# Decay attention and two feed-forward layers: the first activation from the Mish table, weight signs merged on VectorE

## The chip, the cores and the metric

The kernel runs on one core of a Trainium2 chip. The metric is the device time of one execution in microseconds, taken as the median of several runs; lower is better. The matrix engine is TensorE (PE in the profile, its weight loads PEld), the elementwise engines are VectorE (DVE), ScalarE (ACT) and GpSimd (POOL), and SyncE (SP) issues the transfers. Each engine works through its own queue in order, and semaphores make one wait for another.

## What is computed

Three things follow one another. First a causal attention with a decay, over 2 batches of 8 heads, 768 positions of 64 features; its output, put together, is 1536 tokens of 512 features. Then a feed-forward layer with Mish, `h = x @ w_in`, `g = h * tanh(log(1 + exp(h)))`, `g @ w_out`, with 2048 hidden features. Then a second such layer with `g = h * clip(h + 3, 0, 6) / 6`.

```python
def _moe_ref(x, w_in, w_out):
    h = x @ w_in
    sp = np.where(h > 20.0, h, np.log1p(np.exp(np.minimum(h, 20.0))))
    g = h * np.tanh(sp)
    return (g @ w_out).astype(np.float32)
```

The inputs and the result are float32, and the weights come to the chip as float64 bit patterns.

## The kernel before, in words

**Precision.** The large products run on float32r operands. To keep float32 accuracy each operand is split into a rounded high part (`split_hi`, a copy on ScalarE, L67) and the rest (`split_lo`, a subtraction on VectorE, L70). A product is then three matmuls: high by high, high by low, low by high.

**Tiles and steps.** Tokens are cut into three blocks `k` of 512 (X[k]), the hidden features into 16 tiles `t` of 128 (W[t], which holds a tile of the first matrix and of the second). A step `n` of the loop is one pair of layer and (k, t). There are 96 steps, 48 for each layer. In a step `gemm1` (L274, twelve matmuls of 512 columns) makes h for block k and tile t in PSUM, the activation makes g of it, and `gemm2` (L287, twelve matmuls) adds g times the second matrix into four PSUM banks y. The loop is pipelined by hand: in iteration n TensorE gets gemm1(n) and then gemm2(n-2). `act_first(n)` puts the first activation functions on ScalarE in the same iteration; `dve_first(n-1)`, `g_hi(n-1)` and `g_lo(n-1)` come an iteration later. h has two PSUM buffers, so gemm1(n+2) can start when the last reader of h(n) is done.

**The Mish activation before.** With th = tanh(h/2), Mish is a rational function of th. ScalarE makes th (L310), a square of it (L311) and, with Silu and Sin on scaled th (L312, L313), a first value for a reciprocal. VectorE makes a Newton step of it and the product with h (L322, L323, L324). L324 is the last reader of h. ScalarE then makes the high part of g (L334) and VectorE the low part (L342). The second layer uses Relu with a bias on ScalarE (L316), a minimum and product on VectorE (L328), and the plain splits.

**Weights.** A 64-bit pattern is turned into float32 in place in a staging tile `st`. A conversion (`convert`) has for a half of one tile W[t] (512 numbers wide) or of two tiles (1024 wide, seven times, the first ones after two narrow ones): on ScalarE a scaled copy of the high word (L247) and a copy of some low bits (L248); a merge of the sign; on VectorE a shift and merge (L258); then the split into W (L67 on ScalarE, L70 on VectorE). There are 57 conversions. The sign merge is done either on ScalarE (L253, a strided 16-bit write, with L248 writing 16-bit words) or on VectorE (L255, with L248 writing 32-bit words). A hand-written set `on_act` names 27 of the 57 for ScalarE. Two staging tiles alternate; a load of the next one is put on SP's queue (L236) after the conversion that frees its tile.

**Order.** The attention is done in 12 chunks. The first four come ahead of the loop; the others are threaded into iterations 0 to 15 by a table (`att_at`): `scores` makes a score product (L154), `weigh` masks it on VectorE, `attend` makes the outputs (L191, L197, L203), and `settle` moves these on. Another table (`conv_at`) says after which iteration how many conversions are put in, and `conv_first` whether ahead of the activation. The framework's planner may still move an instruction of a queue past others by its own estimate of when things are ready. The last four weight tiles, 12 to 15, lie where the attention's buffers were; each of the three blocks uses tiles 0 to 7 in steps 0 to 23 (block 2 goes on with 8 to 15 up to step 31), blocks 0 and 1 use 8 to 15 in steps 32 to 47, and the second layer runs over all 16 for each block in steps 48 to 95.

**Pools.** `g` (4 KB a partition) has two buffers, tm2 has two each for the tags `x`, `a` and `o` (2 KB), tm1 one for `th`. Output copies (L362) use tags `o` and `a` in turn, four buffers in all; the decay table's `lam_sb` and `pw` sit in `a` and `th`. One activation table set, with the functions of the first layer, is loaded at the start (L425).

Of the kernel before, what the change touches and what calls it, by code (L numbers as in the profile page):

```python
# [15 lines left out]
ALU = mybir.AluOpType  # L16
# [5 lines left out]
def decay_attention__mish_ffn__hswish_ffn_kernel(  # L22
# [18 lines left out]
    g_p = ctx.enter_context(tc.tile_pool(name="g", bufs=2))  # L41
# [21 lines left out]
    def f32(ap):  # L63
        return ap.bitcast(F32)
# [49 lines left out]
    def decay_tables():  # L114
        lam_sb = tm2_p.tile([128, 512], F32, tag="a", name="lam_sb")[0:8, 0:1]
        pw = tm1_p.tile([128, 512], F32, tag="th", name="pw")[0:8, 0:256]
# [187 lines left out]
    def act_first(n):  # L304
        h = h_t[n]
        x = tm2_p.tile([128, 512], F32, tag="x", name="x")
        if seq[n][0] == 0:
            th = tm1_p.tile([128, 512], F32, tag="th", name="th")
            a = tm2_p.tile([128, 512], F32, tag="a", name="a")
            nc.scalar.activation(out=th, in_=h, func=ACTF.Tanh, scale=0.5)  # L310
            nc.scalar.activation(out=x, in_=th, func=ACTF.Square, scale=-0.5, bias=0.5)  # L311
            nc.scalar.activation(out=a, in_=th, func=ACTF.Silu, scale=1.03356325, bias=-3.37153266)  # L312
            nc.scalar.activation(out=a, in_=a, func=ACTF.Sin, scale=-6.86865902, bias=0.1585412)  # L313
            f_t[n] = (x, a)
        else:
            nc.scalar.activation(out=x, in_=h, func=ACTF.Relu, bias=3.0)  # L316
            f_t[n] = x

    def dve_first(n):
        if seq[n][0] == 0:  # L320
            x, y0 = f_t[n]
            nc.vector.scalar_tensor_tensor(out=x, in0=x, scalar=1.0, in1=y0, op0=ALU.add, op1=ALU.mult)  # L322
            nc.vector.scalar_tensor_tensor(out=x, in0=x, scalar=-2.0, in1=y0, op0=ALU.add, op1=ALU.mult)  # L323
            nc.vector.scalar_tensor_tensor(out=x, in0=x, scalar=0.5, in1=h_t[n], op0=ALU.add, op1=ALU.mult)  # L324
            f_t[n] = x
        else:
            r = f_t[n]
            nc.vector.scalar_tensor_tensor(out=r, in0=r, scalar=6.0, in1=h_t[n], op0=ALU.min, op1=ALU.mult)  # L328
        del h_t[n]

    def g_hi(n):
        g = g_p.tile([128, 2, 512], F32R, tag="g", name="g")
        if seq[n][0] == 0:
            nc.scalar.activation(out=g[:, 0], in_=f_t[n], func=ACTF.Copy, scale=-2.0)  # L334
        else:
            split_hi(g[:, 0], f_t[n])
        g_t[n] = g

    def g_lo(n):
        g = g_t[n]  # L340
        if seq[n][0] == 0:
            nc.vector.scalar_tensor_tensor(  # L342
                out=g[:, 1], in0=f_t.pop(n), scalar=-2.0, in1=f32(g[:, 0]), op0=ALU.mult, op1=ALU.subtract
            )
        else:
            split_lo(g[:, 1], g[:, 0], f_t.pop(n))

    def evacuate(n, es):
        layer, k, t, first, last, end = seq[n]
        for e in es:  # L350
# [5 lines left out]
            elif end == "split":  # L356
                split_hi(X[k][:, 0, e, :], y)
                split_lo(X[k][:, 1, e, :], X[k][:, 0, e, :], y)
            else:
                o = tm2_p.tile([128, 512], F32, tag="o" if e % 2 else "a", name="o")  # L360
                r0 = k * 512 + e * 128
                nc.scalar.activation(out=o, in_=y, func=ACTF.Copy, scale=1.0 / 6.0)  # L362
                nc.sync.dma_start(out=out[r0:r0 + 128, :], in_=o)
# [49 lines left out]
    def advance(count):  # L413
# [7 lines left out]
    on_act = {  # L421
        0, 2, 3, 4, 5, 7, 9, 10, 11, 13, 14, 17, 19, 20, 21, 22, 35, 37, 44, 47, 48, 49, 50,
        51, 54, 55, 56,
    }
    nc.scalar.preload_act_table_set("silu_and_others")  # L425
# [146 lines left out]
```

## Time and profile before

| | |
|---|---|
| median of 3 runs | 616.82 us (616.25 to 617.41) |
| span of the profiled execution | 617.7 us |
| time of the profiled execution beyond its span | not given |
| TensorE, share of the span | 96% |
| ScalarE | 63% |
| VectorE | 55% |
| mean granted TensorE clock | 0.986 |

The span goes from the first to the last instruction on the core. Shares of an engine are means over stretches that differ, so they are to be read by stretch. A group of twelve matmuls of 512 columns is the unit of the work on TensorE; matmuls overlap, so the length of a group is best read from its start to the start of the next one.

### The profile page before, as it was taken

The numbers are of one execution on the slowest core, as the hardware profiler recorded it, in microseconds if no ns is written. First come the engines' busy times: TensorE is split into PE (matmuls) and PEld (weight loads), VectorE is DVE, ScalarE is ACT, GpSimd is POOL, SyncE is SP. The second block draws the span as 40 slices with busy tenths as digits, with TensorE's granted clock in tenths as the row PEclk, the third lists the DMA queues.
The fourth block names the chain that finished last, engine by engine and source line by source line (L and its number), as shares of the span: only waits on it lengthen the run. The fifth ranks groups of instructions, "written<-read, shape, count | busy, mean of one in ns | idle before, by whom it ended". The sixth has DMA issues, their size and how long they took to land.

```text
span 617.7 us, 7512 instructions
## 1 busy us (share of the span) xinstructions
PE 594.7 (96%) x2938; PEld 481.0 (78%) x2938; DVE 342.1 (55%) x527; ACT 388.3 (63%) x611; POOL 9.7 (2%) x14
## 2 busy tenths in 40 slices
PE   6989799999998999999999999999999999999997
PEld 3867577888776888878888888788888888888885
DVE  2776678778756888778797675522222222222221
ACT  0699989996899887898688977521322222322212
POOL 1400000000000000000000000000000000000000
PEclk8998899999999999999999999999999999999999
DMA  7935451441212323212212231100100000100001
GB/s 222 409 110 198 152 189 68 137 137 70 102 68 103 103 103 102 103 69 102 70 40 97 102 103 68 35 1 1 68 1 0 1 0 1 69 0 2 0 1 68
DMA packets 15955, 50.56 MB, mean 82 GB/s; under 512 B 1576, under 2 KB 3120, under 8 KB 15920
## 3 DMA queue, kind: packets, MB, share of 16 engines
q1 hardware_dynamic: 15920, 50.08, 23.1%
q8 instruction: 23, 0.38, 0.2%
q14 instruction: 12, 0.10, 0.1%
HBM read 46.92 MB, written 3.15 MB: 81 GB/s over the span
## 4 chain that ended last, share of the span: by engine, by line
PE 55%; ACT 29%; DVE 8%; DMA 5%; issue 3%; POOL 0%; SPq 0%; ACTq 0%; DVEq 0%; POOLq 0%
PE y L287 27%; PE h L274 26%; ACT st L248 6%; ACT st L253 5%; DMA st<-w 3%; ACT st L247 3%; ACT W L67 3%; ACT a L312 2%; ACT x L311 2%; ACT g L334 2%; ACT a L313 2%; ACT th L310 2%; DVE W L70 1%; DVE st L258 1%; ACT X L67 1%
## 5 line engine op out<-in xcount | busy, mean ns | idle before, releaser
L274 PE MATMUL h<-X,W 128*128 128x512 f32 x1152 | 285.2, 397 | 6.9 <-DVE x L324 5.4
L274 PEld LDWEIGHTS h<-X,W 128*128 128x128 f32 x1152 | 216.3, 189 | 58.4 <-DVE x L324 7.8
L287 PE MATMUL y<-g,W 128*128 128x512 f32 x576 | 141.6, 395 | 3.3 <-ACT W L67 2.7
L287 PE MATMUL y<-W,g 128*128 128x512 f32 x576 | 139.5, 391 | 0.1
L287 PEld LDWEIGHTS y<-g,W 128*128 128x128 f32 x576 | 109.0, 190 | 27.9 <-ACT W L67 3.1
L287 PEld LDWEIGHTS y<-W,g 128*128 128x128 f32 x576 | 108.0, 188 | 24.1 <-DVE g L70 0.7
L70 DVE TENSOR_TENSOR g<-x,g 128x512 fp32r<-128x512 f32 x48 | 33.2, 692 | 86.2 <-ACT g L67 86.2
L316 ACT ACTIVATE x<-h 128x512 f32<-128x512 f32 x48 | 28.8, 601 | 82.3 <-PE h L274 82.3
L67 ACT ACTIVATE g<-x 128x512 fp32r<-128x512 f32 x48 | 30.5, 634 | 78.0 <-PE y L287 77.1
L328 DVE SCALAR_TENSOR_TENSOR x<-x,h 128x512 f32<-128x512 f32 x48 | 33.0, 687 | 81.1 <-ACT x L316 81.1
L258 DVE SCALAR_TENSOR_TENSOR st<-st 128x512 int32<-128x512 int32 (+1 forms) x57 | 43.3, 761 | 37.9 <-ACT st L253 37.8
L248 ACT ACTIVATE st<-st 128x512 int32<-128x512 uint16 (+3 forms) x57 | 63.3, 1111 | 0.0
L70 DVE TENSOR_TENSOR W<-st,W 128x512 fp32r<-128x512 f32 (+1 forms) x57 | 43.8, 770 | 20.4 <-ACT W L67 19.6
L247 ACT ACTIVATE st<-st 128x512 f32<-128x512 f32 (+1 forms) x57 | 41.7, 732 | 9.7 <-DMA st<-w 9.6
L67 ACT ACTIVATE W<-st 128x512 fp32r<-128x512 f32 (+1 forms) x57 | 40.9, 719 | 5.7 <-DVE st L258 5.6
L342 DVE SCALAR_TENSOR_TENSOR g<-x,g 128x512 fp32r<-128x512 f32 x48 | 33.2, 691 | 19.1 <-ACT g L334 17.7
L253 ACT ACTIVATE st<-st 128x512 f16<-128x512 f32 (+1 forms) x27 | 42.5, 1576 | 0.4
L310 ACT ACTIVATE th<-h 128x512 f32<-128x512 f32 x48 | 30.0, 624 | 15.9 <-PE h L274 15.8
L334 ACT ACTIVATE g<-x 128x512 fp32r<-128x512 f32 x48 | 30.2, 629 | 9.2 <-DVE x L324 6.8
L322 DVE SCALAR_TENSOR_TENSOR x<-x,a 128x512 f32<-128x512 f32 x48 | 32.9, 686 | 4.9 <-ACT a L313 4.8
L323 DVE SCALAR_TENSOR_TENSOR x<-x,a 128x512 f32<-128x512 f32 x48 | 33.1, 689 | 0.9
L324 DVE SCALAR_TENSOR_TENSOR x<-x,h 128x512 f32<-128x512 f32 x48 | 32.8, 683 | 0.4
(42 smaller groups left out, 328.5 us busy)
## 6 DMA issues: line engine op xcount, KB each, us to landing
st<-w SPq DMA_DIRECT2D x50, 512.0 KB, 3.2
raw<-att SPq DMA_DIRECT2D x24, 512.0 KB, 4.8
st<-w SPq DMA_DIRECT2D x7, 1024.0 KB, 7.3
out<-o SPq DMA_DIRECT2D x12, 256.0 KB, 2.0
mask<-z SPq DMA_DIRECT2D x2, 256.0 KB, 3.9
table<-z SPq DMA_DIRECT2D x2, 128.0 KB, 4.4
lam_sb<-lam SPq DMA_DIRECT2D x1, 0.0 KB
z<-pw SPq DMA_DIRECT2D x1, 8.0 KB
```

What stands on the lines that cost most here:

```text
L67: nc.scalar.activation(out=hi, in_=src, func=ACTF.Copy)
L70: nc.vector.tensor_tensor(out=lo, in0=src, in1=f32(hi), op=ALU.subtract)
L247: nc.scalar.activation(out=hf, in_=hf, func=ACTF.Copy, scale=2.0 ** -112)
L248: nc.scalar.activation(out=lo16[..., 0] if sign_on_act else lo, in_=lo16[..., 1], func=ACTF.Copy, scale=2.0 ** -13, bias=2.0 ** -14 - 0.5,)
L253: nc.scalar.activation(out=sign, in_=hf, func=ACTF.Copy)
L258: nc.vector.scalar_tensor_tensor(out=hi, in0=hi, scalar=3, in1=lo, op0=ALU.logical_shift_left, op1=ALU.bitwise_or)
L274: nc.tensor.matmul(h, lhsT=W[t][:, a, kt * 128:kt * 128 + 128], rhs=X[k][:, b, kt, :], start=(kt, a, b) == order[0], stop=(kt, a, b) == or ...
L287: nc.tensor.matmul(y[e], lhsT=l, rhs=r, start=(first and i == 0), stop=(last and i == 2),)
L310: nc.scalar.activation(out=th, in_=h, func=ACTF.Tanh, scale=0.5)
L323: nc.vector.scalar_tensor_tensor(out=x, in0=x, scalar=-2.0, in1=y0, op0=ALU.add, op1=ALU.mult)
L334: nc.scalar.activation(out=g[:, 0], in_=f_t[n], func=ACTF.Copy, scale=-2.0)
L342: nc.vector.scalar_tensor_tensor(out=g[:, 1], in0=f_t.pop(n), scalar=-2.0, in1=f32(g[:, 0]), op0=ALU.mult, op1=ALU.subtract)
```

## The change

In the first layer the activation reads h twice from PSUM with the Mish function: once into x as float32 and once, rounded, into the high part of g. The low part is the plain subtraction. The four functions, the three VectorE operations and the scaled copy are gone for that layer; the second layer keeps its operations. `g` is now made in `act_first`, an iteration sooner, and has three buffers. The set `on_act` is empty, so all 57 sign merges are done on VectorE and L248 always writes 32-bit words. The tag `a` is gone: the output copies use two buffers of `o`, and `lam_sb` lies in `x`; `th` is half as long. The table set that is loaded at the start is the one with Mish.

```diff
--- before.py
+++ after.py
@@ -38,7 +38,7 @@
     NMID = 2
 
     main = ctx.enter_context(tc.tile_pool(name="main", bufs=1))
-    g_p = ctx.enter_context(tc.tile_pool(name="g", bufs=2))
+    g_p = ctx.enter_context(tc.tile_pool(name="g", bufs=3))
     tm2_p = ctx.enter_context(tc.tile_pool(name="tm2", bufs=2))
     tm1_p = ctx.enter_context(tc.tile_pool(name="tm1", bufs=1))
     dram_p = ctx.enter_context(tc.tile_pool(name="dram", bufs=1, space=DRAM))
@@ -112,8 +112,8 @@
         return rr.to_broadcast([128, 4, 2, 64])
 
     def decay_tables():
-        lam_sb = tm2_p.tile([128, 512], F32, tag="a", name="lam_sb")[0:8, 0:1]
-        pw = tm1_p.tile([128, 512], F32, tag="th", name="pw")[0:8, 0:256]
+        lam_sb = tm2_p.tile([128, 512], F32, tag="x", name="lam_sb")[0:8, 0:1]
+        pw = tm1_p.tile([128, 256], F32, tag="th", name="pw")[0:8, 0:256]
         nc.sync.dma_start(out=lam_sb, in_=lam.unsqueeze(1))
         load_raw(0, 0)
         load_raw(0, 1)
@@ -303,47 +303,28 @@
 
     def act_first(n):
         h = h_t[n]
+        g = g_p.tile([128, 2, 512], F32R, tag="g", name="g")
         x = tm2_p.tile([128, 512], F32, tag="x", name="x")
         if seq[n][0] == 0:
-            th = tm1_p.tile([128, 512], F32, tag="th", name="th")
-            a = tm2_p.tile([128, 512], F32, tag="a", name="a")
-            nc.scalar.activation(out=th, in_=h, func=ACTF.Tanh, scale=0.5)
-            nc.scalar.activation(out=x, in_=th, func=ACTF.Square, scale=-0.5, bias=0.5)
-            nc.scalar.activation(out=a, in_=th, func=ACTF.Silu, scale=1.03356325, bias=-3.37153266)
-            nc.scalar.activation(out=a, in_=a, func=ACTF.Sin, scale=-6.86865902, bias=0.1585412)
-            f_t[n] = (x, a)
+            nc.scalar.activation(out=x, in_=h, func=ACTF.Mish)
+            nc.scalar.activation(out=g[:, 0], in_=h, func=ACTF.Mish)
+            del h_t[n]
         else:
             nc.scalar.activation(out=x, in_=h, func=ACTF.Relu, bias=3.0)
-            f_t[n] = x
+        f_t[n] = x
+        g_t[n] = g
 
     def dve_first(n):
-        if seq[n][0] == 0:
-            x, y0 = f_t[n]
-            nc.vector.scalar_tensor_tensor(out=x, in0=x, scalar=1.0, in1=y0, op0=ALU.add, op1=ALU.mult)
-            nc.vector.scalar_tensor_tensor(out=x, in0=x, scalar=-2.0, in1=y0, op0=ALU.add, op1=ALU.mult)
-            nc.vector.scalar_tensor_tensor(out=x, in0=x, scalar=0.5, in1=h_t[n], op0=ALU.add, op1=ALU.mult)
-            f_t[n] = x
-        else:
+        if seq[n][0] == 1:
             r = f_t[n]
-            nc.vector.scalar_tensor_tensor(out=r, in0=r, scalar=6.0, in1=h_t[n], op0=ALU.min, op1=ALU.mult)
-        del h_t[n]
+            nc.vector.scalar_tensor_tensor(out=r, in0=r, scalar=6.0, in1=h_t.pop(n), op0=ALU.min, op1=ALU.mult)
 
     def g_hi(n):
-        g = g_p.tile([128, 2, 512], F32R, tag="g", name="g")
-        if seq[n][0] == 0:
-            nc.scalar.activation(out=g[:, 0], in_=f_t[n], func=ACTF.Copy, scale=-2.0)
-        else:
-            split_hi(g[:, 0], f_t[n])
-        g_t[n] = g
+        if seq[n][0] == 1:
+            split_hi(g_t[n][:, 0], f_t[n])
 
     def g_lo(n):
-        g = g_t[n]
-        if seq[n][0] == 0:
-            nc.vector.scalar_tensor_tensor(
-                out=g[:, 1], in0=f_t.pop(n), scalar=-2.0, in1=f32(g[:, 0]), op0=ALU.mult, op1=ALU.subtract
-            )
-        else:
-            split_lo(g[:, 1], g[:, 0], f_t.pop(n))
+        split_lo(g_t[n][:, 1], g_t[n][:, 0], f_t.pop(n))
 
     def evacuate(n, es):
         layer, k, t, first, last, end = seq[n]
@@ -357,7 +338,7 @@
                 split_hi(X[k][:, 0, e, :], y)
                 split_lo(X[k][:, 1, e, :], X[k][:, 0, e, :], y)
             else:
-                o = tm2_p.tile([128, 512], F32, tag="o" if e % 2 else "a", name="o")
+                o = tm2_p.tile([128, 512], F32, tag="o", name="o")
                 r0 = k * 512 + e * 128
                 nc.scalar.activation(out=o, in_=y, func=ACTF.Copy, scale=1.0 / 6.0)
                 nc.sync.dma_start(out=out[r0:r0 + 128, :], in_=o)
@@ -418,11 +399,8 @@
                 load_w(*plan[loaded[0]])
                 loaded[0] += 1
 
-    on_act = {
-        0, 2, 3, 4, 5, 7, 9, 10, 11, 13, 14, 17, 19, 20, 21, 22, 35, 37, 44, 47, 48, 49, 50,
-        51, 54, 55, 56,
-    }
-    nc.scalar.preload_act_table_set("silu_and_others")
+    on_act = set()
+    nc.scalar.preload_act_table_set("mish")
     warm_up(10)
     decay_tables()
     load_raw(2, 0)
```

## Rows read from the trace of the kernel before

**Rows 1.** Busy time of each engine over the whole span (the page's first part).

```profile
PE 594.7 (96%) x2938; PEld 481.0 (78%) x2938; DVE 342.1 (55%) x527; ACT 388.3 (63%) x611; POOL 9.7 (2%) x14
```

**Rows 2.** Busy us by stretch: PE, PEld, DVE, ACT, POOL (instructions), PEclk, DMA share, GB/s.

```profile
0.00:31.90 31.90, 24.70 (x242) 19.23 (x242) 16.71 (x35) 12.74 (x26) 9.67 (x14) 0.89 0.87 316
31.90:94.40 62.50, 55.67 (x331) 43.14 (x329) 44.36 (x60) 59.42 (x70) 0.00 (x0) 0.92 0.48 165
94.40:160.70 66.30, 66.30 (x424) 54.25 (x425) 52.59 (x81) 57.74 (x96) 0.00 (x0) 1.00 0.29 99
160.70:393.60 232.90, 227.68 (x986) 184.21 (x984) 171.97 (x270) 201.73 (x331) 0.00 (x0) 1.00 0.25 87
393.60:617.70 224.10, 220.31 (x960) 180.16 (x960) 56.47 (x82) 56.68 (x94) 0.00 (x0) 1.00 0.04 15
```

**Rows 3.** Waits of PE, whole span: us in total, times, longest us.

```profile
PE h L274 <- DVE x L324: 5.4, 7, 1.1
PE y L287 <- ACT W L67: 2.7, 1, 2.7
```

**Rows 4.** Chain that ended last, 31.9 to 94.4 us, shares by line.

```profile
by line: ACT st L248 20.9%; ACT st L253 19.1%; ACT W L67 10.0%; ACT st L247 8.3%; PE y L287 7.0%; ACT a L313 4.2%; ACT a L312 4.2%; DVE st L258 3.9%; ACT x L311 3.9%; ACT th L310 3.8%; ACT g L334 3.2%; ACT state L226 3.0%; issue 2.8%; ACT X
```

**Rows 5.** Timeline of PE, a group after a wait: start us, us, what.

```profile
45.28 5.46 PE L274 MATMUL h<-X,W 128*128 128x512 f32 x12 [0.60 <-DVE x L324]
```

**Rows 6.** Timeline of PE, the full stretch with attention.

```profile
100.09 1.16 PE L154 MATMUL sc<-raw 64*128 64x128 f32 x16
106.85 0.69 PE L191 MATMUL u<-raw 128*64 128x64 f32 x16
109.74 3.00 PE L274 MATMUL h<-X,W 128*128 128x512 f32 x12
...
145.99 1.16 PE L154 MATMUL sc<-raw 64*128 64x128 f32 x16
```

**Rows 7.** Timeline of PE (160.73, 393.56) and the chain's pieces (start us, us, what).

```profile
160.73 2.88 PE L274 MATMUL h<-X,W 128*128 128x512 f32 x12
...
393.56 3.02 PE L274 MATMUL h<-X,W 128*128 128x512 f32 x12 [0.44 <-DVE x L328]
...
201.32 2.72 PE y L287 x12
...
410.18 2.81 PE h L274 x12
```

**Rows 8.** Groups by line and shape: xcount, busy us, mean ns, idle before.

```profile
L253 ACT ACTIVATE st<-st 128x512 f16<-128x512 f32 x22 | 30.0, 1365 | 0.4
L310 ACT ACTIVATE th<-h 128x512 f32<-128x512 f32 x48 | 30.0, 624 | 15.9 <-PE h L274 15.8
L248 ACT ACTIVATE st<-st 128x512 uint16<-128x512 uint16 x22 | 29.8, 1356 | 0.0
L324 DVE SCALAR_TENSOR_TENSOR x<-x,h 128x512 f32<-128x512 f32 x48 | 32.8, 683 | 0.4
L248 ACT ACTIVATE st<-st 128x512 int32<-128x512 uint16 x28 | 18.7, 666 | 0.0
L253 ACT ACTIVATE st<-st 128x1024 f16<-128x1024 f32 x5 | 12.5, 2501 | 0.0
L248 ACT ACTIVATE st<-st 128x1024 uint16<-128x1024 uint16 x5 | 12.6, 2515 | 0.0
L255 DVE SCALAR_TENSOR_TENSOR st<-st 128x1024 int32<-128x1024 int32 x2 | 2.4, 1224 | 0.1
L248 ACT ACTIVATE st<-st 128x1024 int32<-128x1024 uint16 x2 | 2.3, 1140 | 0.0
L425 ACT ACT_TABLE_LOAD x1 | 1.3, 1283 | 0.7 <-PEq L564 0.7
```

**Rows 9.** Loads of wide staging tiles and output stores: KB each, us to landing.

```profile
st<-w SPq DMA_DIRECT2D x7, 1024.0 KB, 7.3
out<-o SPq DMA_DIRECT2D x12, 256.0 KB, 2.0
```

## The prediction, made before the change was run

> **What bounds the kernel now.** I read first the page's busy line [rows 1]: TensorE is busy for 594.7 of 617.7 us, so at first sight only 23.0 us are open. Next I cut the span into five stretches and asked for each engine's busy time in each [rows 2]. The cuts are the first matmul of L274 (31.9), the start of its eighth step (94.4), the end of the attention work (160.7), and the point at which the last weight has been converted (393.6). The reader should compare TensorE with ScalarE: from 31.9 to 94.4 TensorE idles 6.8 us and its granted clock is 0.92 while ScalarE is busy 59.4 of 62.5 us; from 94.4 to 160.7 TensorE never idles; from 160.7 to 393.6 it idles 5.2 us; after 393.6 it is full at clock 1.00 and ScalarE has 56.7 us in 224. TensorE's waits name VectorE's L324, the last of the three Newton and product steps, which frees a buffer of h, and a weight split on ScalarE [rows 3]. The chain of waits inside 31.9 to 94.4 shows what made those late: the two weight conversion lines L248 and L253 take 40.0% of it and the activation lines L310 to L334 over 19%, all on ScalarE [rows 4]. So TensorE bounds the kernel nearly everywhere, and ScalarE bounds it in two places.
>
> Idle time understates the loss, since a matmul at half the clock counts as busy: twelve matmuls of L274 took 5.46 us from 45.28 [rows 5], after a wait, against 2.72 us from start to start in a full stretch [rows 7]. I therefore count by full-speed periods. In the full stretch one score, one attend and two whole steps repeat; three of these periods go from 100.09 to 145.99, 15.30 us each [rows 6]. Between 31.9 and 94.4 lie seven gemm1 and five gemm2 groups, twelve in all, which is three periods' worth (four groups each), with three scores and four attends. The fourth attend is 2.89 us whole (106.85 to 109.74 [rows 6]), but of the four one has no carry and another no state product; I count 1.46 us. Needed: 45.90 + 1.46 = 47.4 us. Taken: 62.5. **Loss one: 15.1 us.** Between gemm1 of step 16 at 160.73 and of step 57 at 393.56 lie 41 steps in 232.83 us [rows 7]. At 5.44 us a step (two groups of 2.72) they need 223.0. Groups on the last four weight tiles take 2.81 instead of 2.72 even in the full stretch (the row at 410.18 [rows 7]); 12 of the 41 steps use those, 24 groups by 0.09, 2.2 us that stay. **Loss two: 232.8 - 223.0 - 2.2 = 7.6 us.**
>
> The Trainium skill (Perfetto Trace Analysis, Identifying the Most-Contended Engine) holds that matmul busy time is a poor measure of headroom and weight-load busy time a better one. By it, 481.0 us of weight loads at the last stretch's share, 180.16 of 224.1, would need 598 us, some 19.5 less than now, where the idle time of the two lossy stretches alone gives 12; the count by periods, 22.7, sides with the rule.
>
> **The change, part by part.**
> *Activation.* Per step of the first FFN ScalarE loses Tanh, Square, Silu, Sin and the scaled copy, five operations like the 0.624 us of L310, and gains two reads of h from PSUM; L310 is such a read, so 1.25 us: 3.12 - 1.25 = 1.87 us less. VectorE loses three operations and keeps one of four, at 0.683 us [rows 8], 2.05 us less. Over 48 steps: ScalarE -90 us, VectorE -98 us. In place of five functions, three VectorE steps and a copy in series there are two functions and one subtraction.
> *What h waits for.* h was freed by L324; now by the second Mish. From the end of gemm1(n) to the start of gemm1(n+2), which needs that buffer, TensorE has three groups, 8.2 us; the pair needs 1.25. The 5.4 us of waits on L324 [rows 3] therefore go, and no other operation takes their place until ScalarE is 6.9 us behind.
> *New waits.* The second Mish writes g at once, so g is held a step longer; the third buffer pays for it: the buffer that g(n) takes was read by gemm2(n-3), issued ahead of gemm1(n). x(n) waits for the subtraction of step n-2, as before. Cost nothing, covered by the 8.2 us.
> *Signs.* Of 27 sign merges on ScalarE five are 1024 wide, 2.50 us each, and 22 are 512 wide, 1.37 us. With the merge on VectorE, L248 also writes whole words: 2.52 becomes 1.14 us at 1024, 1.36 becomes 0.67 at 512. ScalarE: 5 x 3.88 + 22 x 2.06 = 65 us less. VectorE: 5 x 1.22 + 22 x 0.69 = 21 us more (the narrow ones priced like L324) [rows 8].
> *By stretch.* From 31.9 to 94.4, seven steps and five wide conversions: ScalarE 59.4 - 13.1 - 19.4 = 26.9 us, VectorE 44.4 - 14.4 + 6.1 = 36.1, against TensorE's need of 47.4. From 160.7 to 393.6, 32 steps and 16 conversions: ScalarE 201.7 - 59.8 - 33.0 = 109, VectorE 172.0 - 65.6 + 11.0 = 117, against 225. Neither engine can bound either stretch by its sum.
> *What is late next.* Weights. A wide conversion is six operations in series (three on each engine) of about 1.14 to 1.22 us, 7.1 us; its load of 1 MB lands after 7.3 us [rows 9]; two staging tiles alternate, and SP issues the next load only when the conversion two earlier has released its tile. That is 14.4 us for two conversions, 7.2 each, where TensorE needs the seven wide ones spread over its 47 us, 6.8 each, with two already loaded at the start. It just about keeps pace. I leave 3 of the 15.1 us there: bounds 0 (conversions always ahead) and 7.5 (half of the loss stays). Loss one gives 12.1 us.
> *Loss two* came from h and from ScalarE behind loads of 512 KB; I leave 0.6, bounds 0 and 3.8, since a conversion in ScalarE's queue still can hold a Mish until its load lands. Gain 7.0 us. No DMA is added or moved; loads start sooner as conversions end sooner.
> *Ahead of 31.9* the first conversion, narrow, stands among the first attention chunks: ScalarE loses 1.37 + 0.69 = 2.06 us, VectorE, busy too, gets 0.69. No row tells how much is on the path: bounds -2.06 and +0.69; I take the middle, -0.7.
> *Output and set-up.* Output copies alternate over two buffers instead of four, so the third of each four waits for the first one's transfer, 2.0 us [rows 9] less the copies between. The banks that they read are wanted a gemm1 later, 2.72 us. Taken 0, bound +1.3 for two places. lam and pw only change their tiles: 0.
> *Sum:* 617.7 - 0.7 - 12.1 - 7.0 = 597.9 us. This is against the profiled execution, of which only the span, 617.7, is given; the runs' median is 616.82, 0.14% less. Scaled so: **597.0 us**.
>
> **Rivals.**
> *Weights stay late.* The two-tile round trip just reckoned, or VectorE's three operations per conversion behind one another, keeps half of loss one, and loads keep half of loss two. For it: 14.4 us per pair is close to the need, and ScalarE already waits in its queue for splits. Against it: ScalarE's 40% of the chain [rows 4] is mostly the part that shrinks. 617.7 - 7.5 - 3.8 = 606.4, on the median 605.5.
> *Slower: table switches.* There is one table load now, 1.283 us, for a set with all four functions [rows 8]. If the Mish table came without Copy or Relu, each passage between Mish and a copy would cost a load on ScalarE. ScalarE has 319 us of work from 31.9 to 393.6 and loses 155, so it has room for 198 us, 154 loads, 3.2 per step. Two per step would leave it near no gain, since each stands ahead of a Mish; at four per step, as conversions are threaded between, 246 us, it would overrun by 48: 666 us. The Trainium skill (ScalarE: Activation LUTs, Table sets: the hidden batching unit) says that cheap functions, copy and relu among them, are in every set as filler, by which this does not happen; it does not list a set with Mish, and no row before shows one.
> *Nothing moves.* The same waits remain by another name, for example because ScalarE's queue, ordered by the planner, sits behind loads in both stretches: about 617. Against it: ScalarE's sums fall by half, and after 94.4, where it is busy 87% and not behind, TensorE never waits.
>
> **How the numbers follow.** Forecast 0.67; weights stay late 0.25; nothing moves 0.03; slower 0.05, most of it the switches. What a measurement here tells from no change is about 0.2%, 1.2 us. Faster 0.92, same 0.03, slower 0.05. The low end takes every best bound: 617.7 - 2.1 - 15.1 - 7.6 = 592.9, on the median 592. The high end is the first rival with the worst bounds of the opening and the outputs, 605.5 + 0.7 + 1.3 = 607.5. The range 592 to 607.5 leaves out the last two cases and little more.
>
> **What would show it.** Right: in the changed profile ScalarE about 27 us busy in the first seven steps and TensorE's granted clock there near 1.00; no wait of L274 on an activation step; that stretch about 50 us long; gemm1 of step 16 to step 57 about 226 us; from there to the end as before, 224 us. Weights late shows as waits of L274 and L287 on W. Switches show as more than one table load. The forecast is wrong if the stretch from 31.9 keeps over 55 us, or if the opening grows.

## The result, and the profile after

The changed kernel took **598.45 us** (median of 4 runs, 597.28 to 599.25), the kernel before on the same chip 617.12 (616.25 to 617.78). The ratio is **0.9686**, 95% interval 0.9657 to 0.9715: faster by 3.1%. The prediction was 597.0, in a range of 592 to 607.5. The profiled execution has a span of 596.9 us and took 599.02 in all, so about 2.1 us lie around the span.

The busy line of the page, as in [rows 1]:

```profile
PE 585.4 (98%) x2938; PEld 477.1 (80%) x2938; DVE 277.8 (47%) x410; ACT 255.8 (43%) x440; POOL 9.7 (2%) x14
```

ScalarE lost 132 us and VectorE 64; TensorE's instructions are the same in number and 9.3 us shorter in busy time. That alone does not explain a span that is 20.8 us shorter, so the stretches come next, cut at the same matmuls as [rows 2] (start, first matmul of L274, the start of its eighth step, the end of the attention work, the start of step 57). The columns are those of [rows 2]:

```profile
0.00:31.40 31.40, 23.86 (x242) 18.37 (x242) 17.52 (x36) 10.97 (x25) 9.69 (x14) 0.95 0.89 320
31.40:81.50 50.10, 49.93 (x331) 39.74 (x330) 43.11 (x52) 35.27 (x50) 0.00 (x0) 1.00 0.57 200
81.50:147.70 66.20, 66.20 (x426) 54.16 (x425) 39.12 (x59) 32.41 (x61) 0.00 (x0) 1.00 0.32 111
147.70:373.00 225.30, 225.30 (x985) 184.80 (x984) 123.96 (x187) 122.20 (x215) 0.00 (x0) 1.00 0.26 88
373.00:596.90 223.90, 220.13 (x961) 180.08 (x959) 54.07 (x79) 54.99 (x90) 0.00 (x0) 1.00 0.04 15
```

Read the first number behind each colon against [rows 2]: 31.4 for 31.9, **50.1 for 62.5**, 66.2 for 66.3, **225.3 for 232.9**, 223.9 for 224.1. The two stretches named in the prediction gave 20 of the 20.8 us. In both TensorE is now busy from end to end but for 0.2 us, and in the second row its granted clock is 1.00 (the 2.4 GHz level) where it was 0.92. The same matmuls fill 49.93 us there instead of 55.67 [rows 2]: groups at half clock, like the one of [rows 5], are gone, and this difference of 5.7 us is most of the 9.3.

TensorE's waits over the whole span (total us, times, longest), which answer to [rows 3]:

```profile
PE o L197 <- DVE amat L179: 4.5, 2, 3.3
PE sc L154 <- DMA raw<-att: 1.4, 1, 1.4
PE wp L84 <- DVE wz L81: 1.2, 1, 1.2
PE u L191 <- POOL raw L170: 0.5, 1, 0.5
PE y L287 <- ACT W L67: 0.2, 1, 0.2
```

All but the last belong to the opening. The 5.4 us on the last Newton step are gone, and of the 2.7 us on a weight split 0.2 is left. The chain of waits inside 31.4 to 81.5, by line, answers to [rows 4]:

```profile
by line: PE h L274 30.7%; PE y L287 22.8%; PE o L197 11.3%; PE sc L154 6.7%; PE o L203 6.5%; DVE st L258 4.6%; ACT W L67 4.6%; PE u L191 2.5%; DVE st L255 2.4%; ACT st L248 2.1%; DVE X L70 1.4%; ACT X L67 1.2%; DVE amat L179 1.2%; ACT x L30
```

It ran through ScalarE's conversion lines before; now TensorE's own matmuls are most of it. The groups by line and shape (count, busy us, mean ns, idle before) price the new operations:

```profile
L309 ACT ACTIVATE x<-h 128x512 f32<-128x512 f32 x48 | 28.5, 594 | 57.2 <-PE h L274 57.2
L310 ACT ACTIVATE g<-h 128x512 fp32r<-128x512 f32 x48 | 28.4, 592 | 0.0
L248 ACT ACTIVATE st<-st 128x1024 int32<-128x1024 uint16 x7 | 8.0, 1147 | 0.0
L403 ACT ACT_TABLE_LOAD x1 | 1.3, 1283 | 0.7 <-PEq L542 0.7
```

A Mish costs 0.593 us whether it writes float32 or the rounded part, and there is one table load, as before. Below, "0-7" is the stretch from gemm1 of step 0 to gemm1 of step 7, "16-57" that from step 16 to step 57; they are the second and fourth rows above.

### The profile page after: what moved, and what is told of

Read it like the earlier page. It is cut to its first block, busy times and chain, and to the rows that moved or that the text cites. A ratio compares the mean times of both kernels' runs of the same rounds, so it can differ in the third digit from the quotient of the medians.

```text
span 596.9 us, 7267 instructions
## 1 busy us (share of the span) xinstructions
PE 585.4 (98%) x2938; PEld 477.1 (80%) x2938; DVE 277.8 (47%) x410; ACT 255.8 (43%) x440; POOL 9.7 (2%) x14
## 4 chain that ended last, share of the span: by engine, by line
PE 94%; DVE 2%; DMA 2%; ACT 1%; issue 0%; POOL 0%; SPq 0%; POOLq 0%; ACTq 0%
PE y L287 44%; PE h L274 44%; PE o L197 3%; PE o L203 2%; PE sc L154 2%; PE u L191 1%; DMA mask<-z 1%; DMA z<-pw 1%; DVE st L258 0%; ACT W L67 0%; DVE st L255 0%; DVE pw L126 0%; DVE W L70 0%; DVE X L70 0%; DMA lam_sb<-lam 0%
## 5 line engine op out<-in xcount | busy, mean ns | idle before, releaser
L274 PE MATMUL h<-X,W 128*128 128x512 f32 x1152 | 281.4, 393 | 0.0
L274 PEld LDWEIGHTS h<-X,W 128*128 128x128 f32 x1152 | 215.1, 188 | 47.6
L70 DVE TENSOR_TENSOR g<-x,g 128x512 fp32r<-128x512 f32 x96 | 66.2, 690 | 76.4 <-ACT g L310 46.7
L320 DVE SCALAR_TENSOR_TENSOR x<-x,h 128x512 f32<-128x512 f32 x48 | 33.0, 687 | 144.1 <-ACT x L313 144.0
L313 ACT ACTIVATE x<-h 128x512 f32<-128x512 f32 x48 | 28.8, 599 | 144.3 <-PE h L274 144.3
L255 DVE SCALAR_TENSOR_TENSOR st<-st 128x512 int32<-128x512 int32 (+1 forms) x57 | 43.5, 764 | 32.8 <-ACT st L248 32.7
L67 ACT ACTIVATE W<-st 128x512 fp32r<-128x512 f32 (+1 forms) x57 | 41.2, 725 | 36.1 <-DVE st L258 36.1
L70 DVE TENSOR_TENSOR W<-st,W 128x512 fp32r<-128x512 f32 (+1 forms) x57 | 44.0, 773 | 23.8 <-ACT W L67 21.7
L247 ACT ACTIVATE st<-st 128x512 f32<-128x512 f32 (+1 forms) x57 | 41.9, 735 | 28.8 <-DMA st<-w 26.7
L309 ACT ACTIVATE x<-h 128x512 f32<-128x512 f32 x48 | 28.5, 594 | 57.2 <-PE h L274 57.2
L67 ACT ACTIVATE g<-x 128x512 fp32r<-128x512 f32 x48 | 30.3, 632 | 32.2 <-DVE x L320 32.0
L258 DVE SCALAR_TENSOR_TENSOR st<-st 128x512 int32<-128x512 int32 (+1 forms) x57 | 43.2, 758 | 1.6
L248 ACT ACTIVATE st<-st 128x512 int32<-128x512 uint16 (+1 forms) x57 | 41.1, 721 | 0.0
L310 ACT ACTIVATE g<-h 128x512 fp32r<-128x512 f32 x48 | 28.4, 592 | 0.0
L197 PE MATMUL o<-amat,raw 128*64 128x128 f32 x192 | 21.3, 285 | 4.6 <-DVE amat L179 4.5
L197 PEld LDWEIGHTS o<-amat,raw 128*64 128x64 f32 x192 | 17.6, 142 | 6.6 <-DVE amat L179 4.9
L179 DVE TENSOR_TENSOR amat<-sc,mask 128x512 f32<-128x512 f32 x24 | 16.1, 685 | 11.4 <-DMA mask<-z 8.8
```

Source lines behind the costliest of these rows:

```text
L67: nc.scalar.activation(out=hi, in_=src, func=ACTF.Copy)
L70: nc.vector.tensor_tensor(out=lo, in0=src, in1=f32(hi), op=ALU.subtract)
L197: nc.tensor.matmul(o[h2 * 64:h2 * 64 + 64, p, :], lhsT=vn[:, h * 64:h * 64 + 64], rhs=amat[h2][:, p, :], start=(p == 0), stop=(last and p ...
L247: nc.scalar.activation(out=hf, in_=hf, func=ACTF.Copy, scale=2.0 ** -112)
L248: nc.scalar.activation(out=lo16[..., 0] if sign_on_act else lo, in_=lo16[..., 1], func=ACTF.Copy, scale=2.0 ** -13, bias=2.0 ** -14 - 0.5,)
L255: nc.vector.scalar_tensor_tensor(out=lo, in0=hi, scalar=-2 ** 31, in1=lo, op0=ALU.bitwise_and, op1=ALU.bitwise_or)
```

## The experiments

The prediction rested on a theory of **load**: ScalarE's sum of work bounded the two stretches. Three rivals stand against it: **release** (the buffer of h came free late), **round trip** (in 0-7 a wide conversion and its load, over two staging tiles, take too long whatever the engines' sums) and **queue** (in 16-57 one operation held in an engine's in-order queue makes others late). The edits are against the changed kernel, except the second. Every kernel ran beside the kernel before (618.5 to 620.0 us in these groups), and ratios are to that. The runs are called e1 to e12; they stand here by subject.

**One part at a time.** First the Mish alone, with the signs left as they were:

```diff
-    on_act = set()
+    on_act = {0, 2, 3, 4, 5, 7, 9, 10, 11, 13, 14, 17, 19, 20, 21, 22, 35, 37, 44, 47, 48, 49, 50, 51, 54, 55, 56}
```

> The changed kernel, but the 27 sign merges stand on ScalarE as before; it computes the same. Load theory (ScalarE's sum of work bounded the two stretches): from the first gemm1 to that of step 7 ScalarE has 59.4 - 13.1 = 46.3 us of work against TensorE's need of 47.4, so it stays nearly full and 5 to 8 of the 15.1 us remain; from step 16 to step 57 it has 142 of 225 us and under 1 us remains: 603 to 607. Release theory (h was freed late because five functions and three VectorE steps stood in series): all of the gain is here, 598 to 600. Conversion theory (only the late weights cost time): over 610.

This is e1: 624.76 us, ratio 1.009 (1.0056 to 1.0123): **0.9% slower than the kernel before**, and outside every forecast but the last. Its windows for 0-7 and 16-57, and the main waits of TensorE (as above):

```profile
31.70:93.00 61.30, 53.97 (x330) 42.47 (x329) 36.73 (x46) 51.78 (x55) 0.00 (x0) 0.92 0.49 160
...
160.30:397.80 237.50, 230.28 (x985) 187.45 (x984) 114.14 (x172) 149.84 (x230) 0.00 (x0) 0.98 0.25 84
```

```profile
PE y L287 <- ACT W L67: 6.6, 2, 4.0
PE y L287 <- DVE part L336: 3.6, 1, 3.6
PE y L287 <- DVE X L70: 3.2, 1, 3.2
```

In 0-7 ScalarE (fourth busy time) has 7.6 us less to do than before [rows 2], and the stretch is only 1.2 us shorter. So ScalarE's sum was not what held most of that stretch back. In 16-57 the stretch is 4.7 us longer than before, with less work on both engines.

Next the signs alone, made from the kernel before:

```diff
-    on_act = {0, 2, 3, 4, 5, 7, 9, 10, ..., 56}
+    on_act = set()
```

> The kernel before, but all 57 sign merges on VectorE; it computes the same. Load theory: ScalarE 40 us and VectorE 50.5 us in the first stretch against 47.4, so VectorE becomes the full one and 5 to 8 us of loss one remain; 169 and 183 of 225 us in the later stretch leave 1 to 3 us of loss two: 604 to 609. Release theory: the series is as long as before, 612 to 617. Conversion theory: 599 to 603.

This is e2: 604.34 us, ratio 0.9772 (0.9743 to 0.98): 14.7 of the roughly 20 us, and inside the load theory's forecast. Its windows for 0-7 and 16-57:

```profile
31.40:87.50 56.10, 51.46 (x345) 41.08 (x343) 53.25 (x69) 46.63 (x69) 0.00 (x0) 1.00 0.56 191
...
153.10:378.50 225.40, 225.40 (x986) 184.84 (x985) 180.56 (x287) 174.28 (x313) 0.00 (x0) 1.00 0.27 89
```

In 16-57 the signs alone bring the whole gain, with ScalarE still at 174 us, far over the 122 of the changed kernel. In 0-7 they leave 6 us. There VectorE (third busy time), with the signs and the Newton steps on it, is busy 53.25 of 56.1, and TensorE waits 2.8 us for L324, the last of these steps. That fits a bound by VectorE's load, and it fits h held too long as well; no run parts the two. The two parts of the change don't add: the Mish is a loss alone and pays 6 us on top of the signs.

**Load by itself.** Four dead copies behind each Mish pair give ScalarE back much of its old load, with no sign among it:

```diff
+            junk = tm1_p.tile([128, 512], BF16, tag="junk", name="junk")
+            for _ in range(4):
+                nc.scalar.activation(out=junk, in_=x, func=ACTF.Copy)
```

> The changed kernel with four copies of x into a scratch tile put on ScalarE right behind each Mish pair, so that h is freed as in the changed kernel and the load is put back (about 2.5 us a step). Load theory: ScalarE 35.3 + 17.5 = 53 us in the first stretch, over the need of 47.4, which takes 55 to 60 us; 122 + 80 = 202 us in the later one, as before the change, where 4 to 8 us come back: 606 to 616. Release theory: 598 to 600, since h is freed no later.

This is e3: 598.87 us, ratio 0.9669 (0.9648 to 0.9691). The windows of 0-7 and 16-57:

```profile
31.10:81.50 50.40, 50.40 (x330) 40.31 (x329) 40.88 (x50) 46.52 (x73) 0.00 (x0) 1.00 0.60 199
...
147.70:373.00 225.30, 225.30 (x985) 184.90 (x984) 124.69 (x187) 186.85 (x345) 0.00 (x0) 1.00 0.27 88
```

ScalarE (fourth busy time) is at 92% and 83% of the two stretches, near the 95% and 87% of the kernel before, and nothing is slower. In 0-7 less load came back than was meant (46.5 us against 53). That is under TensorE's need of 47.4, so the load theory itself expects no loss from it, and for this stretch e1 says more. For 16-57 it says more: in steps 16 to 28, where 5.1 of the 7.5 us were lost, ScalarE is busy 59.3 of 65.3 us (91%), against 64.8 of 70.4 (92%) before, and nothing is lost. And the 64.8 us of before are themselves under the 65.3 that TensorE takes, so ScalarE's sum was not what bounded there.

**Release by itself.** h is kept until VectorE has read it, as it was before:

```diff
-            del h_t[n]
...
+        if seq[n][0] == 0:
+            junk = tm1_p.tile([128, 512], BF16, tag="junk", name="junk")
+            nc.vector.tensor_copy(junk, h_t.pop(n))
```

> The changed kernel with a copy of h into a scratch tile on VectorE an iteration after the Mish pair, where the product with h stood, so that h is held as long as before and little load is added (0.69 us a step on VectorE). Load theory: 598 to 602, the upper part if VectorE, 43.1 + 4.8 us of 50.1 in the first stretch, delays splits there. Release theory: the waits of gemm1 on a VectorE step come back in both stretches, 606 to 612.

This is e4: 600.3 us, ratio 0.9698 (0.9678 to 0.9718). 0-7 took 51.7 us instead of 50.1, 16-57 the same 225.34, and TensorE never waits for a buffer of h. The added copies fill VectorE to 46.69 us in 0-7.

This run doesn't refute the release theory, since h is not held nearly as long in it as before. In steps 16 to 47 the time from the end of gemm1(n) to the end of the last read of h is at most 3.0 us here and was up to 10.3 us before, and TensorE wants the buffer again after three groups, about 8.2 us. The trace of before speaks for release in 16-57. All of TensorE's waits there are:

```profile
PE h L274 <- DVE x L324: 4.6, 5, 1.1
PE h L274 <- DVE x L328: 0.4, 1, 0.4
```

The five on L324 follow releases 8.9 to 10.3 us after the end of gemm1. With the signs alone moved (e2) the latest release in steps 16 to 47 comes after 7.6 us, with the Mish alone (e1) the latest in steps 16 to 28 after 6.9, and no wait on h is left in either place. The longest of before's waits, 1.14 us, is for h of step 20. Its gemm1 on TensorE, and pieces of the chain that leads from there to the wait's end (start us, us, what):

```profile
185.04 2.88 PE L274 MATMUL h<-X,W 128*128 128x512 f32 x12
```

```profile
185.58 4.26 DMA st<-w
...
190.54 1.23 ACT st L248
191.77 0.43 ACT th L310
...
193.75 1.26 ACT st L253
...
197.57 0.69 DVE x L324
...
198.31 3.02 PE h L274 x12
```

gemm1 of step 20 ended at 187.92, but its first function, L310, starts only at 191.77. Ahead of it on ScalarE stand the first operations of a conversion whose load had just landed, and a sign merge (L253) follows before VectorE's steps. So this h was late by what stood in ScalarE's queue at that time.

In 0-7 release was the smaller part. Waits on L324 were 0.8 of 6.8 us of idle time there before, and e1 frees h 4.2 us after gemm1 in the mean, in place of 12.1, for the 1.2 us said above.

**The wide signs and the narrow ones apart.** Only the five wide conversions' signs go back to ScalarE, then only the 22 narrow ones:

```diff
-    on_act = set()
+    on_act = {2, 3, 4, 5, 7}
```

> The changed kernel with only the five wide sign merges back on ScalarE; it computes the same. Round-trip theory: a wide conversion is 9.9 us in place of 7.1, with a load of 7.4 half a round trip is 8.6, seven are 60: first stretch 59 to 62 us, the rest as in the changed kernel: 607 to 610. Load theory: ScalarE 35 + 19 = 54 us in a need of 47: 54 to 56 us, 602 to 605.

This is e8: 609.58 us, ratio 0.9841 (0.9819 to 0.9862). All of the loss lies in 0-7, 60.6 us; 16-57 is 225.34 again. The round-trip forecast holds. The window of 0-7, then TensorE's main wait there:

```profile
30.90:91.50 60.60, 53.30 (x330) 42.14 (x329) 36.67 (x46) 51.66 (x55) 0.00 (x0) 0.94 0.50 166
```

```profile
PE y L287 <- ACT W L67: 6.6, 2, 4.0
```

ScalarE is busy 51.66 of 60.6 us, VectorE 36.67: neither is full, and yet five signs cost 10.5 us. What grew is the length of a conversion. From the ends of the seven wide conversions in the trace (the last L70 of each), the spacing is (82.3 - 41.6) / 6 = 6.8 us in the changed kernel, (93.8 - 42.4) / 6 = 8.6 here and (99.9 - 44.5) / 6 = 9.2 before. Seven of those make 47.5, 60.0 and 64.6 us, against 50.1, 60.6 and 62.5 for the stretch. The spacing by itself proves little, since whatever makes the steps late spreads the conversions too (in e3 it is (85.5 - 41.6) / 6 = 7.3 us, and nothing is lost). Two things say more. The forecast of 59 to 62 us was made from the chain beforehand, where load gave 54 to 56. And here one staging tile never rests: its conversions run from 31.9 to 42.4, 49.6 to 62.2, 70.2 to 78.7 and 86.0 to 93.8, and its next load goes out within 0.1 us of the end of each; the gaps of 7.2 to 7.9 us are about what a load takes [rows 9]. Meanwhile TensorE waits for weights. That SP's loads hang on the conversions shows in the waits of its queue, in the changed kernel from 31 to 93:

```profile
SPq L236 <- DVE W L70: 27.4, 6, 8.1
```

Six loads of staging tiles waited for the last operation of an earlier conversion. The narrow signs:

```diff
-    on_act = set()
+    on_act = {0, 9, 10, 11, 13, 14, 17, 19, 20, 21, 22, 35, 37, 44, 47, 48, 49, 50, 51, 54, 55, 56}
```

> The changed kernel with the 22 narrow sign merges back on ScalarE and the wide ones left on VectorE; it computes the same. Round-trip theory (the first stretch lasts as long as seven wide conversions over two staging tiles, half of load plus conversion each): the first stretch is 50 to 51 us as in the changed kernel, and from step 16 to step 57 the narrow ones bring back the 12 us of the run with all 27 there: 609 to 612. If the narrow ones do no harm by themselves: 598 to 600.

This is e7: 613.54 us, ratio 0.99 (0.9861 to 0.994). Now 0-7 is whole, 50.11 us, and 16-57 takes 238.0, a little over the forecast. The loss sits in two places, at gemm2 of steps 32 and 48:

```profile
PE y L287 <- DVE part L336: 3.6, 1, 3.6
PE y L287 <- DVE X L70: 3.3, 1, 3.3
```

**A longer conversion without more load.** GpSimd is idle there; a copy in place on it, 1.28 us in the mean, stands inside each wide conversion:

```diff
         if count == 2:
+            nc.gpsimd.tensor_copy(hf, hf)
```

> The changed kernel with one more step in series in each wide conversion, on GpSimd, which has nothing else to do there: a copy in place of the 1024 numbers, about 1.5 to 2.5 us, ahead of the split. ScalarE and VectorE get no work. Round-trip theory: half of it for each of seven, the first stretch grows by 4 to 9 us: 602 to 607. Load theory: no change, 598 to 599. If conversions had slack in the changed kernel, the growth is under half of that.

This is e9: 601.14 us, ratio 0.9706 (0.9686 to 0.9726), between the two forecasts. The window of 0-7:

```profile
31.10:83.40 52.30, 51.18 (x330) 39.91 (x329) 40.98 (x50) 33.81 (x49) 7.55 (x6) 1.00 0.58 193
```

ScalarE and VectorE have less to do there than in the changed kernel, and the stretch is 2.3 us longer; every other stretch is the same. The spacing of conversions went from 6.8 to (88.5 - 42.4) / 6 = 7.7 us. This is half of what 1.28 us per conversion would cost if nothing had slack (seven halves, 4.5 us, since two tiles alternate). VectorE's operations on a wide tile are as long as in the changed kernel (1.22 us each), so the copy doesn't slow them; what was added is length of the chain. So the round trip costs here, and the changed kernel stands close to where it begins to.

**The two stalls of the narrow signs.** In e1 the trace around the first stall, all engines (start us, us, what, [idle before <- releaser]):

```profile
262.52 0.65 ACT L247 ACTIVATE st<-st 128x512 f32<-128x512 f32 x1 [1.92 <-DMA st<-w]
263.08 0.63 ACT L248 ACTIVATE st<-st 128x512 int32<-128x512 uint16 x1
263.62 0.58 ACT L309 ACTIVATE x<-h 128x512 f32<-128x512 f32 x1
264.09 0.59 ACT L67 ACTIVATE X<-y 128x512 fp32r<-128x512 f32 x1
...
265.05 1.58 ACT L67 ACTIVATE X<-y 128x512 fp32r<-128x512 f32 x3
265.82 4.61 PE L287 MATMUL y<-g,W 128*128 128x512 f32 x12 [3.22 <-DVE X L70]
```

The last line is TensorE, at gemm2 of step 32, waiting for the four y banks that the copies X<-y empty. Those stand on ScalarE behind the beginning of conversion 42 (counted from 0), which waited 1.92 us for its load. It is in no hurry: its split into W comes only at 307.5 us, 45 us later. The other stall, at gemm2 of step 48, has the additions of L336 on VectorE in the place of the copies. In the changed kernel the first place reads:

```profile
243.73 0.60 ACT L309 ACTIVATE x<-h 128x512 f32<-128x512 f32 x1 [1.16 <-PE h L274]
244.22 0.59 ACT L310 ACTIVATE g<-h 128x512 fp32r<-128x512 f32 x1
244.70 1.09 ACT L67 ACTIVATE X<-y 128x512 fp32r<-128x512 f32 x2
```

The copies follow the Mish pair at once. To test this, the signs of e7 were kept, and the conversions that ran ahead were put behind the bank copies in the order of their engine:

```diff
+        ins = nc.scalar.activation(out=hf, in_=hf, func=ACTF.Copy, scale=2.0 ** -112)
+        if done[0] in (41, 42):
+            behind(ins, emptied["split"])
...
+        if done[0] in (52, 53):
+            behind(ins if sign_on_act else sgn, emptied["add"])
```

> The run with the wide signs on VectorE and the narrow ones on ScalarE, and nothing but the order of four conversions changed: the first ScalarE operation of conversions 41 and 42 stands behind the copies that empty the y banks after step 31, and the first VectorE operation after ScalarE's of conversions 52 and 53 behind the additions that empty them after step 47. It computes the same. Queue theory (the 12 us come from bank copies that stand in a queue behind conversions waiting for a load or for a sign): the wait of gemm2 on the X split, 3.3 us, goes, and most of the wait on the addition, 3.6 us; steps 28 to 40 fall from 72.5 to 67 or 68, steps 48 to 57 from 55.9 to 50 to 53: 600 to 605. If the narrow signs' own work is what costs, as in the kernel before: no change, 612 to 614.

This is e10: 606.89 us, ratio 0.9823 (0.9788 to 0.9859), 16-57 231.75, a little above the forecast: half came back, and waits of 3.0 and 2.0 us were left. The trace shows why the first stayed:

```profile
251.09 0.65 ACT L259 ACTIVATE st<-st 128x512 int32<-128x512 uint16 x1 [2.51 <-DMA st<-w]
...
252.59 2.07 ACT L67 ACTIVATE X<-y 128x512 fp32r<-128x512 f32 x4
```

A conversion begins with two operations that each need only the load. The first (L247 in the changed kernel) was moved; the second (L248, here L259) had stayed in front and took the wait. With both moved, and at the second stall also conversion 51 and the products of steps 49 and 50:

```diff
+        if done[0] in (41, 42):
+            behind(ins, emptied["split"])
+            behind(low, emptied["split"])
...
+        if done[0] in (51, 52, 53):
+            behind(ins if sign_on_act else sgn, emptied["add"])
...
+            if n in (49, 50):
+                behind(ins, emptied["add"])
```

> As the run with the banks emptied first, with the gaps of its order closed: of conversions 41 and 42 both first ScalarE operations stand behind the copies after step 31 (there the second one had gone ahead and waited for the load in their place), and behind the additions after step 47 stand the VectorE operation of conversion 51 too, and the products with h of steps 49 and 50. It computes the same; 22 narrow signs are still on ScalarE. Queue theory: both waits go, steps 28 to 40 at 66.6 to 67.5 us, steps 48 to 57 at 49 to 51, 599 to 602. If the narrow signs' work is what costs: these stretches stay at 70 and 51 or more, 605 and up.

This is e12: 600.79 us, ratio 0.971 (0.9689 to 0.9731). The window of 16-57:

```profile
148.20:373.80 225.60, 225.60 (x985) 184.76 (x985) 113.55 (x172) 149.39 (x230) 0.00 (x0) 1.00 0.26 89
```

Both waits are gone, and 16-57 is back at 225.6 us **with all 22 narrow signs still on ScalarE**: 12.4 us came back from order alone. So those stalls were the queue, not the work. Against the changed kernel 2.3 us of span are left, in the opening (0.8), steps 7 to 16 (0.5), 16-57 (0.2) and the end (0.85).

**Two small questions.** Does g need its third buffer?

```diff
-    g_p = ctx.enter_context(tc.tile_pool(name="g", bufs=3))
+    g_p = ctx.enter_context(tc.tile_pool(name="g", bufs=2))
```

> The changed kernel with two buffers of g in place of three, so that the second Mish of step n must wait for gemm2 of step n-2, which TensorE does right behind gemm1(n); it computes the same. By the prediction's slack (three groups, 8.2 us, from gemm1(n) to the next use of h's buffer; this wait takes one group of them): no change, 597 to 600. If the third buffer is what makes room: waits of gemm1 on the second Mish, over 603.

This is e11: 598.42 us, ratio 0.9674 (0.9654 to 0.9694): it does not. And do the groups on the last four weight tiles take longer because of where those tiles start? A pad moves them by 32 and by 64 bytes:

```diff
+    pad_p = ctx.enter_context(tc.tile_pool(name="pad", bufs=1, side="right"))
+    pad_p.tile([128, 8], F32, name="pad")
```

> The changed kernel with a pad of 32 bytes a partition ahead of everything on the right side of SBUF. Weight tiles 12 to 15 then start at a multiple of 64 bytes, like all the other weight tiles; now they start 32 bytes past one. Start theory (the 2.81 us of their groups, against 2.72, come from where they start): all groups take 2.72, 48 groups by 0.085 us are 4.1 us less: 594 to 595, and the attention tiles, which share the side, may give a little more. Other theory (the groups are slow for another reason, such as which part of SBUF they lie in): no difference, 598.5.

> The same with a pad of 64 bytes: the tiles move further, but still start 32 bytes past a multiple of 64. Start theory: 598.5, groups of tiles 12 to 15 at 2.81 us. Other theory, if any move helps: less than 598.

These are e5 and e6: 598.45 (0.9665, 0.9646 to 0.9684) and 598.21 us (0.966, 0.9641 to 0.9678): no difference. Pieces of the chain in the first of them (start, us, what), to hold against the 2.81 us of [rows 7]:

```profile
385.99 2.72 PE y L289 x12
388.71 2.80 PE h L276 x12
```

The slow groups stay at 2.80 us. The start of the tiles is not the reason, and what is stays open. None of the twelve kernels is faster than the changed one by more than its interval.

## Why the prediction was right, and which step was not

The forecast of 597.0 us was 1.45 short. The sum itself, 597.9 of span, was 1.0 too long (596.9); what made it short is the scaling by 0.14% "on the median", which put the median 0.9 us below the span, where it came out 1.55 above. That the number came out so well owes something to luck. The sum took back what TensorE lost in the two stretches, and that is the same whatever caused the loss; and the change removed the true causes together with the one that was named.

- *Stage by stage.* "About 50 us" for 0-7: 50.1. "About 226" for 16-57: 225.3. 224 for the rest: 223.9. Opening -0.7: -0.5. Counting the need by whole periods, not by TensorE's idle time, gave the size: the idle time of both stretches was 12 us, the gain 20. The Trainium skill (Perfetto Trace Analysis, Identifying the Most-Contended Engine) prefers weight-load busy time over matmul busy time as a measure of headroom; worked out by that rule the estimate was 598 us, and the trace agrees, 596.9 of span.
- *Activation.* The pair was priced at 1.25 us and takes 1.19. One table load of 1.283 us remains, so the rival of table switches, forecast at 666, is out.
- *What h waits for.* As said, the waits on L324 went and nothing took their place. In 16-57 this step names the cause: these waits and the one on L328 were all of TensorE's idle time there, 5.1 us as listed. In 0-7 they were a small part of it.
- *New waits.* Cost nothing, as forecast; the reason given, that "the third buffer pays for it", is not needed: two buffers cost nothing either (e11).
- ***By stretch* is the step that failed in its reasoning.** It took ScalarE's sum as the bound of both stretches, and the change as a cut of that sum. By its own terms the Mish takes more from ScalarE over the whole kernel than the signs (90 us and 65), and alone it is slower (e1). In 0-7, where the signs are the larger cut (19.4 and 13.1), e1 took 7.6 us off ScalarE and gained 1.2. What bounded there was the length of a wide conversion over two staging tiles (e8, e9): the two 16-bit writes of 2.5 us in [rows 8] stood in series in it. With the signs away from ScalarE 6 us are left there, which the Mish takes away; whether VectorE's sum or the late release makes them stays open (e2). In 16-57 what bounded was the late release of h. Either part alone removes the old loss in steps 16 to 28 (65.3 us in e1 and in e2, for 70.4), the signs alone remove the rest, and ScalarE's load without a late release costs nothing (e3). The Trainium skill (Perfetto Trace Analysis, Identifying the Most-Contended Engine) takes occupancy as a fair measure of how close ScalarE is to its roofline and says to optimize the engine with the highest one first. In this case a stretch with ScalarE at 92% lost nothing, and one with it at 85% (e8) lost 10.5 us.
- *By stretch, the sizes.* 35.3 and 43.1 us came out for 26.9 and 36.1 on ScalarE and VectorE in 0-7, 122 and 124 for 109 and 117 in 16-57. On ScalarE three things were mis-sized. The terms took "seven steps" of five functions, 35, where the trace of before has 30 in the stretch, since the last ones fall behind its end. The shorter stretch holds seven wide splits of W where the longer one had six. And the terms subtracted whole durations from a busy time in which neighbours overlap: in the timeline above the Mish pair starts 0.49 us apart and takes 0.60 and 0.59. The groups of the stretch add up to 38.8 us for 35.27 busy. On VectorE it is the stretch's edges alone: of the Newton steps 18 fell into it and not 21, and after the change it holds one more sign merge than reckoned and a split of W, a shift and two subtractions for g more than before.
- *What is late next.* The 3 us left for late weights was the right size, 50.1 against 47.4, and the wrong cause: TensorE waited 0.2 us for a weight, and in e3 it is busy 50.40 of 50.40 us. Counted from the start of each matmul to the start of the next, what the stretch holds comes to 47.5 us at the pace of the full stretch, so the need was counted rightly. The 2.5 us more in the changed kernel lie on the scores (1.1), gemm1 (0.7), the attention outputs (0.4) and gemm2 (0.2), in a stretch where attention and feed-forward groups are cut finer; why these take longer there, no run shows. The round trip itself, reckoned at 7.2 us a conversion, came out at 6.8, close to the edge as forecast (e9).
- *Loss two.* That it "came from h and from ScalarE behind loads" is what the trace of before shows for its longest wait. The remainder of 0.6 us was nearly nothing here. But the mechanism named for it, a conversion that holds ScalarE's queue until its load lands, is the one that cost e1 and e7 over 12 us, where it held bank copies and not a Mish.
- *Output.* The copies did wait for earlier transfers, and the end is 15.2 us as before: cost 0, as forecast.

## What to carry to other kernels

An engine that is 95% busy in a lossy stretch isn't yet its bound: look for the chain that alternates over a few buffers, add up its length, and compare that with the spacing of the consumer; then test by putting the load back without the chain. Where a wait names the step that frees a buffer, compare how late the buffer comes free with when it is wanted again; a test that delays it less than that shows nothing. Two edits that relieve the same engines can't be priced apart, and one of them may lose alone. Where an in-order queue empties the banks that the next block needs, keep work that waits for a load, and that nobody wants yet, behind those copies.

## What the runs showed that was not expected

- A conversion's first operations on ScalarE, waiting 1.9 us (e1) and 2.5 us (e10) for a load, were enough to stop TensorE for 3.2 and 3.0 us, although the weight goes into W only 45 us later (e1). The Trainium skill (Perfetto Trace Analysis, Sequencer Loop) describes that an instruction waits in its engine's queue for its semaphores; the trace agrees, and e12 shows what the order is worth: 12.4 us.
- Waits cost more than their length: in e8 two waits on weights, 6.6 us together, went with a granted clock of 0.94 in 0-7 and with 10.5 us, where the changed kernel has 0.2 us of waits at 1.00. The same matmuls fill 53.30 us there and 49.93 here. In e7 the waits of 3.3 and 3.6 us went with granted clocks of 0.98 in steps 28 to 40 and 0.94 in steps 48 to 57 and cost 5.9 and 6.8 us; in e10 those of 3.0 and 2.0 us, at 1.00 in both stretches, cost 4.1 and 2.3.
- Groups on the last four weight tiles take 2.80 us instead of 2.72 whether or not these tiles are moved by 32 or 64 bytes.
- Neighbours on ScalarE overlap by a tenth of a microsecond: in the rows above, operations of 0.60 and 0.59 us that follow each other start 0.49 us apart. A sum of means is an upper bound of what an engine's busy time loses.
